# A DiT block on one core: x2 kept in the output tensor, DRAM sums released by weight loads, one more quarter by seven products, ten more constant matmuls

## The chip, the cores and the metric

The kernel runs on one core of a Trainium2 chip. The metric is the device time in microseconds of one execution. A core has a matrix engine (TensorE, PE in the profile), a vector engine (VectorE, DVE), a scalar engine (ScalarE, ACT), a general engine (GpSimd, POOL) and a queue engine (SyncE, SP). SP, ACT and POOL issue transfers. Each engine works through its own list of instructions in order and waits on semaphores that the others raise.

## What is computed

The input x has 2048 rows of 1024 values in bfloat16. One block with conditioned layer norms is applied: linear attention, then a gated feed-forward layer with 3584 hidden columns.

```python
mod = (_silu(c) @ w_mod).reshape(c.shape[0], 6, 1, -1)
sa, ca, ga, sb, cb, gb = (mod[:, 0].copy(), ...)
h = _layernorm(x, axis=-1) * (1 + ca) + sa
x = x + ga * _A_ref(h, A_wqkv, A_wo)          # linear attention, 32 heads
h = _layernorm(x, axis=-1) * (1 + cb) + sb
x = x + gb * _B_ref(h, B_w_gate, B_w_up, B_w_down)
# _B_ref: _gelu(x @ w_gate) * (x @ w_up) @ w_down
```

The x after the attention is called x2 in the kernel; the last line adds the gated feed-forward result to it.

## The kernel before, in words

**Stages.** The rows are taken in four blocks of 512 (TG), and in the feed-forward part in two groups of 1024 (g = 0 and 1). In order of time: the front (`start_phase`, to about 30 us: layer norm of the first block, the modulation columns, the first values of V), K, V and Q with the attention sums (`kvq_phase`, `merge_phase`), the output projection (`wo_phase`), then gate_up(0), down_out(0), gate_up(1), down_out(1). In the profile gate_up(0) lies at about 237 to 407 us, down_out(0) at 403 to 487, gate_up(1) at 482 to 657, down_out(1) from 653 to the end.

**Seven products.** Most products of matrices cut both operands into quarters and form the result from seven quarter products in place of eight, with sums of quarters (s1 to s4 of the activations, t1 to t4 of the weights) prepared beforehand. Some of the seven are cut once more in the same way; they are called nested.

**The down stage.** `down_out(g)` forms seven products with the quarters b11, b21, b22 of w_down and with sums of these quarters, t0 to t3. `nested(name, ...)` does one of them by seven smaller products of 98 matmuls of 256 columns in all (line 2015); `plain(name, ...)` does it directly with 56 matmuls of 512 columns (line 1966) from one load of the whole quarter. In group 0 t1, t2 and t3 are plain, in group 1 only t3 is. `W_AT` (line 1912) names the place in SBUF of each piece, in units of 3.5 KB, and so which earlier piece must be done before a load can be issued. `added` makes the result tile and its `send`, an accumulating store that GpSimd issues (line 1936): it adds to x2. `c22_out`, `c22_quads`, `c21_out`, `c21_last`, `u2_out` are what VectorE does with each finished part in PSUM.

**x2.** `wo_tile` and `wo_stages` write x2 to four DRAM tiles, `x2_scr` (line 766), which `late_norm` reads for group 1's layer norm and `send` adds to. When all eight pieces of a half are sent, line 1942 copies that half, 1 MB, from `x2_scr` to the output; there are three such copies, since the last half is read back (`rest`, line 1950), finished in SBUF and stored by ScalarE's queue (`store`, line 1955).

**Sums in DRAM.** The nested quarters need sums of pieces of w_down. Those of b21, b22 and t0 are made on VectorE (`wd_sums`), that of b11 too (`wd_first`). Those of t2 and t1 (`LATER[1:]`) are made by GpSimd's transfers alone: a plain transfer and then accumulating ones into `v_scr`, eight moves of 448 KB for each (`wd_later`, line 1400). `wd_moves(seen_of, n)` (line 1346) paces them: GpSimd copies one element of `seen_of` into `seen`, which waits until that tile is written and until the last matmul recorded so far is done, and issues the next n moves. Before the change all sixteen are recorded in gate_up(1), two a unit, with `seen_of` in the unit's s1, which VectorE writes.

**Units of gate_up.** A unit is 512 columns of w_gate or w_up, 14 in a group: a load of 1 MB (line 1688), sums on VectorE, matmuls at lines 1729 and 1740. While unit n is multiplied, unit n + 1 (`w_next`) is loaded and summed.

**Order.** Nothing is issued as it is written. `Plan` records all operations, orders them by a planner, and then moves each engine's instructions by the list `SHIFTS` (one number for each instruction: how far it is moved). `Plan.lines` (line 238) tells which bytes an operation touches, which gives the dependences; DRAM scratch is told apart in pieces of 512 elements, inputs and outputs not at all.

**Front.** `keep_warm(n)` (line 900) issues n matmuls of a constant with 512 columns, whose result nobody reads. `scale_cols` (line 930) forms scale columns from w_mod by 32 matmuls of one column, whose weights come in two loads; `scale_wv` multiplies the weights of V by them on VectorE (line 916), and `v_plain` (line 924) multiplies.

Of the kernel before, what the change touches and what calls it, by code (L numbers as in the profile page):

```python
# [11 lines left out]
BF16 = mybir.dt.bfloat16  # L12
F16 = mybir.dt.float16
AF = mybir.ActivationFunctionType
ALU = mybir.AluOpType
# [194 lines left out]

class Op:
    __slots__ = ("extra", "eng", "fn", "args", "kw", "line", "cost", "bytes", "table", "preds", "succs", "early", "late", "due", "ready", "wait", "lat", "needs",
                 "start", "done", "n", "load", "ahead")

class Plan:

# [2032 lines left out]
```

## Time and profile before

| | us |
|---|---|
| median of 3 runs | 738.51 |
| lowest and highest | 737.21, 738.55 |
| the profiled execution's own time | 738.93 |
| its span, first to last instruction | 737.1 |
| granted TensorE clock, mean | 0.996 |

In the lists below a row begins with its start and length in us, or with the stretch and its length; then the engine, the line of the kernel, the operation, what it writes and reads, how many were merged (x), and in brackets the idle time of the engine ahead of it with what ended it. "PEld" is the loading of weights into TensorE, "SPq", "ACTq" and "POOLq" are the sequencers that issue transfers.

### The profile page before, as it was taken

To read this page: it belongs to the slowest core of one execution; us is meant where nothing else is said; L and a number is where in the kernel's file an instruction comes from. 1 tells how busy PE (TensorE), PEld (TensorE's weight loads), DVE (VectorE), ACT (ScalarE), POOL (GpSimd) and SP (SyncE) were. 2 spreads that over 40 slices of the span, in tenths; PEclk is the share of its full clock that TensorE was granted. 3 is DMA by queue.
4 is the path that set the end of the run, shared out by engine and by line. 5 is a ranking of instruction groups with operands and counts; after the bars stand their busy time and mean duration, and the time that the engine had idled before them with its cause. 6 is when DMAs were issued, how large, how long until landed. Compare 5 with 4: busy or idle time off the path is not lost.

```text
span 737.1 us, 12351 instructions
## 1 busy us (share of the span) xinstructions
PE 721.4 (98%) x4463; PEld 413.0 (56%) x4463; DVE 652.3 (88%) x1442; ACT 460.2 (62%) x838; POOL 132.0 (18%) x205
## 2 busy tenths in 40 slices
PE   8999999999999999999999999999989999999996
PEld 4344445444444555555555877455545555568884
DVE  5699998889799999999999994887787999989997
ACT  5486566679687799999877632036757777651220
POOL 2242715011031032222110000131222200000110
PEclk9999999999999999999999999999999999999999
DMA  9877569989999797577968997676869733599987
GB/s 310 298 209 232 139 142 188 325 314 280 314 276 266 264 264 242 188 212 216 235 205 215 265 283 236 196 139 202 190 153 195 144 103 115 159 259 280 284 256 199
DMA packets 177277, 165.70 MB, mean 225 GB/s; under 512 B 34768, under 2 KB 157776, under 8 KB 176656
## 3 DMA queue, kind: packets, MB, share of 16 engines
q1 hardware_dynamic: 150208, 120.08, 55.8%
q0 software_dynamic: 25440, 43.52, 23.7%
q10 hardware_dynamic: 1568, 1.31, 0.6%
q8 instruction: 35, 0.57, 0.3%
q14 instruction: 26, 0.21, 0.1%
HBM read 130.68 MB, written 44.70 MB: 238 GB/s over the span
## 4 chain that ended last, share of the span: by engine, by line
PE 87%; DMA 6%; DVE 4%; issue 1%; POOL 1%; ACT 0%; SPq 0%; DVEq 0%
PE psum L1729 31%; PE psum L2015 13%; PE psum L1740 10%; PE psum L1157 7%; PE psum L1227 6%; PE psum L1966 5%; PE psum L1256 3%; PE psum L1609 3%; PE psum L1543 3%; DVE mem L789 3%; PE psum L924 2%; DMA mem<-in_B_w_up_dram 2%; DMA mem<-ts 1%; DMA mem<-in_B_w_gate_dram 1%; DMA mem<-in_B_w_down_dram 1%; DMA mem<-in_w_mod_dram 1%
## 5 line engine op out<-in xcount | busy, mean ns | idle before, releaser
L789 DVE TENSOR_TENSOR mem<-mem 128x256 f16<-128x256 f16 (+14 forms) x823 | 374.4, 498 | 16.3 <-DMA mem<-in_B_w_up_dram 3.8
L1729 PE MATMUL psum<-mem 128*128 128x512 f16 x1144 | 272.1, 379 | 0.0
L1094 ACT ACTIVATE mem<-psum 128x512 f32<-128x512 f32 (+3 forms) x324 | 170.0, 554 | 116.5 <-PE psum L2015 41.7
L789 DVE TENSOR_TENSOR mem<-psum,mem 128x512 f16<-128x512 f32 (+5 forms) x221 | 164.7, 752 | 31.7 <-ACT mem L1094 11.7
L1729 PEld LDWEIGHTS <-mem 128*128 128x128 f16 (+1 forms) x1144 | 111.8, 98 | 104.2 <-issue 0.6
L2015 PE MATMUL psum<-mem 128*128 128x256 f16 (+1 forms) x980 | 108.6, 273 | 0.0
L1740 PE MATMUL psum<-mem 128*128 128x256 f16 x742 | 105.1, 273 | 3.5 <-DVE psum L789 3.5
L2015 PEld LDWEIGHTS <-mem 128*128 128x128 f16 x980 | 95.9, 98 | 13.0
L1740 PEld LDWEIGHTS <-mem 128*128 128x128 f16 (+1 forms) x742 | 72.5, 98 | 43.5 <-issue 4.4
L1157 PE MATMUL psum<-mem 128*128 128x512 f16 (+1 forms) x280 | 63.3, 379 | 0.7 <-ACT mem L1094 0.7
L1785 ACT ACTIVATE psum<-psum 128x512 f32<-128x512 f32 x56 | 32.8, 586 | 45.8 <-PE psum L1729 33.9
L1936 POOL DMA_DIRECT2D x2s<-mem x12 | 15.6, 1496 | 210.9 <-DVE mem L789 207.2
L789 DVE TENSOR_TENSOR psum<-psum,mem 128x256 f32<-128x256 f32 x106 | 44.9, 429 | 9.4 <-ACT mem L1094 6.9
L1227 PE MATMUL psum<-mem 128*128 128x512 f16 x224 | 51.8, 379 | 0.0
L1966 PE MATMUL psum<-mem 128*128 128x512 f16 (+2 forms) x252 | 49.6, 355 | 1.0 <-DMA mem<-ts 1.0
L1157 PEld LDWEIGHTS <-mem 128*128 128x128 f16 x280 | 26.8, 98 | 32.8 <-DVE mem L1053 1.3
L1804 ACT ACTIVATE mem<-psum 128x512 f16<-128x512 f32 x56 | 33.4, 599 | 8.0 <-PE psum L1729 7.8
L1966 PEld LDWEIGHTS <-mem 128*128 128x128 f16 x252 | 23.5, 98 | 25.1 <-issue 1.2
L1227 PEld LDWEIGHTS <-mem 128*128 128x128 f16 (+1 forms) x224 | 21.5, 98 | 25.6 <-issue 1.0
L1814 ACT ACTIVATE mem<-mem 128x512 f16<-128x512 f16 x56 | 34.8, 630 | 0.0
L1256 PE MATMUL psum<-mem 128*128 128x512 bf16 x128 | 29.5, 379 | 1.0 <-DVE mem L1029 0.8
L1543 PE MATMUL psum<-mem 128*128 128x512 f16 x128 | 28.4, 379 | 0.0
(148 smaller groups left out, 619.4 us busy)
## 6 DMA issues: line engine op xcount, KB each, us to landing
mem<-in_B_w_gate_dram SPq DMA_DIRECT2D x14, 1024.0 KB, 5.4
mem<-in_B_w_up_dram SPq DMA_DIRECT2D x14, 1024.0 KB, 5.1
mem<-in_w_mod_dram SPq DMA_DIRECT2D x24, 512.0 KB, 6.5
mem<-us SPq DMA_DIRECT2D x24, 448.0 KB, 6.8
mem<-in_B_w_down_dram SPq DMA_DIRECT2D x18, 448.0 KB, 6.8
ts<-in_B_w_down_dram POOLq DMA_DIRECT2D x28, 256.0 KB, 5.9
mem<-vs SPq DMA_DIRECT2D x16, 448.0 KB, 6.7
mem<-ts SPq DMA_DIRECT2D x4, 1792.0 KB, 11.7
```

The lines of the kernel that those rows point to most:

```text
L789: ve.tensor_tensor(out=out, in0=a, in1=b, op=op)
L1094: ac.activation(out=t, in_=ps, func=AF.Copy)
L1157: te.matmul(ps, lhsT=A[:, k, i * P:(i + 1) * P], rhs=B[:, k, :], start=(start and k == 0), stop=(k == KH - 1), skip_group_check=True)
L1227: te.matmul(o, lhsT=W[:, k, (j0 + i) * P:(j0 + i + 1) * P], rhs=h_form(a, k), start=(start and k == 0), stop=(k == KH - 1), skip_group_che ...
L1256: te.matmul(ps, lhsT=hr1[b][:, k, tl * P:(tl + 1) * P], rhs=Wk[:, k, n * NW:(n + 1) * NW], start=(k == 0), stop=(k == KD - 1))
L1543: te.matmul(psw[:, half, :], lhsT=pqT[b][:, g, tl * P:(tl + 1) * P], rhs=Wp[:, g, half * NW:(half + 1) * NW], start=(g == 0), stop=(g == K ...
L1729: te.matmul(ps, lhsT=a[:, k, e, :], rhs=b[:, k, :], start=(start and k == 0), stop=(k == KH - 1), skip_group_check=True)
L1740: te.matmul(ps, lhsT=self.x[a][:, k, :], rhs=self.y[y][:, k, :], start=(start and k == 0), stop=(k == KH // 2 - 1), skip_group_check=True)
L1804: ac.activation(out=o, in_=ps, func=AF.Gelu_apprx_tanh)
L1814: ac.activation(out=o, in_=o, func=AF.Gelu_apprx_tanh)
L1966: te.matmul(psm[:, b, c], lhsT=A[:, i, q * P:(q + 1) * P], rhs=wt[:, i, c], start=(start and i == 0), stop=(i == NPR - 1), skip_group_chec ...
L2015: te.matmul(ps[:, q, :], lhsT=a[:, k, q * P:(q + 1) * P], rhs=y[:, k, :], start=(start and q == 0 and k == 0), stop=(k == NPR // 2 - 1), s ...
```

## The change

x2 is kept in the output: the four views that `wo_tile`, `wo_stages`, `late_norm`, `send` and `rest` use are rows of the output tensor, and the copies go. The planner now tells the output apart in pieces of 128 elements. In group 0 t2 is nested, as it is in group 1 already: the sums of A21 go to three places at 144 KB (`sub_d`), `c22_quads` gets a `send`, and t3 adds the part that `c22_quads` leaves in `p5v`. A plain quarter is loaded in two halves. The eight moves for t2 are recorded in gate_up(0) and the eight for t1 in gate_up(1), one a unit at the units in `MOVE_AT`, with `seen_of` in the raw weights of the next unit, which SP's load writes. `keep_warm(2)` becomes `keep_warm(8)`, and a `keep_warm(4)` is added behind the scale columns. `SHIFTS` is another list for every engine, so that all engines have another order in most stages.

```diff
-        if name.startswith("in_") or name.startswith("out_"):
+        if name.startswith("in_"):
             got = ()
         else:
-            unit = 512 * isz
+            unit = (P_OUT if name.startswith("out_") else 512) * isz
...
+    sub_d = [at(144 + 3.5 * j, [NPR // 2, HB], F16) for j in range(3)]
...
-    x2_scr = [scr_pool.tile([TG, D], BF16, name=f"x2s{b}", tag=f"x2s{b}") for b in range(NG)]
+    x2_scr = [o_dram[b * TG:(b + 1) * TG, :] for b in range(NG)]
...
-        keep_warm(2)
+        keep_warm(8)
         scale_cols(0, 0, KH, psc[0])
         scale_cols(0, KH, KD, psc[0])
+        keep_warm(4)
         start_tile(1, xh[1])
...
+    MOVE_AT = ((0, 1, 2, 3, 4, 5, 6, 11), (1, 2, 3, 4, 5, 6, 7, 8))
...
-            if g and n == 0:
-                wd_todo.extend(wd_later())
-            if g and n:
-                wd_moves(w["s1"][:, 0, 0, 0:1], 2)
-            if g == 0 and n % 2 == 0:
-                if n and n // 2 + EARLY - 1 < NPR // 2:
-                    fill += wd_sums(n // 2 + EARLY - 1)
-                wd_moves(w["s1"][:, 0, 0, 0:1], 2)
+            if n == 0:
+                wd_todo.extend(wd_later(LATER[g + 1]))
+            if n in MOVE_AT[g]:
+                wd_moves(w_next["a11"][:, 0, 0, 0:1], 1)
+            if g == 0 and n % 2 == 0 and n and n // 2 + EARLY - 1 < NPR // 2:
+                fill += wd_sums(n // 2 + EARLY - 1)
...
-             "b22": (7, 8, 9, 10, 4, 5, 6), "t2": 0, "t3": 11},
+             "b22": (10, 1, 2, 7, 8, 9, 6), "t2": (3, 4, 0, 5, 10, 1, 2), "t3": 11},
...
-                sent[half] += hi - lo
-                if sent[half] == 2 * TT:
-                    r = (2 * g + half) * TG
-                    gp.dma_start(out=o_dram[r:r + TG, :], in_=x2_scr[2 * g + half])
...
-            sy.dma_start(out=wt, in_=wd_full[name])
+            for c in (slice(0, NPR // 2), slice(NPR // 2, NPR)):
+                sy.dma_start(out=wt[:, c], in_=wd_full[name][:, c])
...
         def u2_out(q, ps, c):
-            t = w12[:, q, :]
-            tt_op(t, p5v[:, q, :], ps, ALU.subtract)
-            tt_op(t, t, gbrow[:, NW:D], ALU.mult)
+            tt_op(p5v[:, q, :], p5v[:, q, :], ps, ALU.subtract)
+            tt_op(w12[:, q, :], p5v[:, q, :], gbrow[:, NW:D], ALU.mult)
...
-        def c22_quads(x2, x1):
+        def c22_quads(x2, x1, send=None):
...
+                if send is not None:
+                    tt_op(quad(x2, r, c), t, gate2(1, c), ALU.mult)
+                    if (r, c) in ((1, 0), (0, 1)):
+                        send(2 * r, 2 * r + 2)
+                    return
...
         def c21_out(xt, send):
             def out(q, ps, c):
-                finish(xt, 0, q, ps, None)
+                t = c0_ring()
+                tt_op(t, ps, gbrow[:, 0:NW], ALU.mult)
+                tt_op(xt[:, q], t, p5v[:, q, :], ALU.add)
...
-            m7 = plain("t2", A21, c22_out(*added(1, 1)), False)
-            run(*m7[:2], n3[5], *m7[2:4], n3[6], *m7[4:])
-            run(*plain("t3", A22, c21_out(*added(1, 0)), False))
+            sub_sums(A21, sub_d, None, [slice(0, NPR // 2)])
+            x2, send = added(1, 1)
+            n7 = nested("t2", A21, sub_d, None, c22_quads(x2, None, send))
+            run(n7[0], n3[5], n7[1], n3[6], *n7[2:5])
+            m8 = plain("t3", A22, c21_out(*added(1, 0)), False)
+            run(m8[0], n7[5], m8[2], n7[6], m8[1], *m8[3:])
```

`wd_later(name)` is now given one name and returns its eight moves, in the order o0, o0 +=, o2, o1, o2 +=, o1 +=, o3, o3 +=.

More of the change, by code (lines that the diff above doesn't have):

```diff
@@ L213 @@
                  "start", "done", "n", "load", "ahead")
+P_OUT = 128
 class Plan:
@@ L1398, in wd_first, with wd_later @@
         gp.dma_start(out=v_scr[:, c, 0], in_=v)
-    def wd_later():
-        todo = []
-        for name in LATER[1:]:
-            v = v_scr[:, :, LATER.index(name)]
-            w = wd_full[name].rearrange("p (i e) (h n) -> p e h i n", e=2, h=2)
-            o0, o1, o2, o3 = (v[:, :, f] for f in range(4))
-            todo.append([(o0, w[:, 0, 0], 0), (o2, w[:, 0, 1], 0), (o0, w[:, 0, 1], 1), (o2, w[:, 1, 1], 1),
-                         (o1, o0, 0), (o1, w[:, 1, 1], 1), (o3, o1, 0), (o3, w[:, 1, 0], 1)])
-        a, b = todo
-        return [*a[:2], *b[:2], *a[2:4], *b[2:4], *(m for pair in zip(a[4:], b[4:]) for m in pair)]
+    def wd_later(name):
+        v = v_scr[:, :, LATER.index(name)]
+        w = wd_full[name].rearrange("p (i e) (h n) -> p e h i n", e=2, h=2)
+        o0, o1, o2, o3 = (v[:, :, f] for f in range(4))
+        return [(o0, w[:, 0, 0], 0), (o0, w[:, 0, 1], 1), (o2, w[:, 0, 1], 0), (o1, o0, 0), (o2, w[:, 1, 1], 1),
+                (o1, w[:, 1, 1], 1), (o3, o1, 0), (o3, w[:, 1, 0], 1)]
     def kvq_phase():
@@ L1938, in send @@
                     in_=xt[:, lo:hi], accum_op=ALU.add)
-                sent[half] += hi - lo
-                if sent[half] == 2 * TT:
-                    r = (2 * g + half) * TG
-                    gp.dma_start(out=o_dram[r:r + TG, :], in_=x2_scr[2 * g + half])
             return xt, send
-        sent = [0, 0]
         def rest(half, nh, xt=None):
@@ L2047, in nested @@
             return [g1, g2, g3, g4, g5, g6, g7]
-        def finish(xt, nh, q, ps, sb, op=ALU.add):
-            gb = gbrow[:, nh * NW:(nh + 1) * NW]
-            if sb is not None:
-                t = c0_ring()
-                tt_op(t, sb, ps, op)
-                ps = t
-            tt_op(xt[:, q], ps, gb, ALU.mult)
         def quad(v, r, c):
@@ L2126, in c12_out @@
             return out
-        def c22_out(xt, send):
-            def out(q, ps, c):
-                finish(xt, 1, q, ps, p5v[:, q, :], ALU.subtract)
-                if q % 2:
-                    send(q - 1, q + 1)
-            return out
-        def c22_quads(x2, x1):
+        def c22_quads(x2, x1, send=None):
             def out(r, c, ps, sb, op):
```

355 rows, old and new, of the table SHIFTS are left out of this document.

## The prediction

> **What bounds the kernel now.** I read first the page's busy shares and the chain of waits, then busy time by stretch, then the few rows in which TensorE stands still.
>
> ```profile
> span 737.1 us, 12351 instructions
> PE 721.4 (98%) x4463; PEld 413.0 (56%) x4463; DVE 652.3 (88%) x1442; ACT 460.2 (62%) x838; POOL 132.0 (18%) x205
> PE 87%; DMA 6%; DVE 4%; issue 1%; POOL 1%; ACT 0%; SPq 0%; DVEq 0%
> ```
>
> ```profile
> 20.00:40.00 20.00, 18.98 (x111) 7.72 (x110) 13.81 (x36) 11.08 (x17) 6.74 (x14) 1.00 0.76 262
> 40.00:90.00 50.00, 49.34 (x274) 23.53 (x273) 47.88 (x118) 32.93 (x47) 22.42 (x41) 1.00 0.71 195
> 165.00:230.00 65.00, 64.72 (x340) 28.91 (x339) 57.85 (x102) 52.21 (x84) 11.92 (x20) 1.00 1.00 283
> 230.00:405.00 175.00, 174.51 (x994) 96.90 (x993) 169.89 (x428) 150.25 (x300) 29.90 (x45) 1.00 0.78 229
> 405.00:457.00 52.00, 51.02 (x425) 41.37 (x424) 44.52 (x76) 23.38 (x38) 0.00 (x0) 1.00 0.94 266
> 457.00:510.00 53.00, 53.00 (x275) 26.69 (x273) 39.59 (x87) 14.22 (x31) 10.61 (x11) 1.00 0.68 178
> 510.00:585.00 75.00, 72.02 (x419) 40.74 (x418) 61.62 (x153) 52.50 (x113) 21.46 (x22) 1.00 0.77 174
> 655.00:714.00 59.00, 59.00 (x536) 52.29 (x535) 58.26 (x90) 13.73 (x25) 2.47 (x2) 1.00 1.05 289
> ```
>
> Each row gives a stretch and its length, then busy time of PE, PEld, DVE, ACT and POOL, the granted clock, the share of the DMA engines and GB/s. From 20 us on TensorE lacks 1.02 + 0.66 + 0.28 + 0.49 + 0.98 + 2.98 = 6.41 us in the rows shown that have a gap. The program is bound by its matmuls; a gain is either a matmul less, one of these gaps, or the two ends. VectorE is the second limit: 97% in gate_up(0) (169.89 of 175) and 99% in the last down stage (58.26 of 59).
>
> **The change part by part.** The sum is made against the profiled execution's 738.93 us, that is its span and 1.8 us around it; it lies 0.42 us above the median, 738.51, and that is taken off at the end.
>
> *(a) t2 of group 0 by seven products.* The plain quarter is 4 x 14 = 56 matmuls of 512 columns; nested it is 7 x 14 = 98 of 256.
>
> ```profile
> 457.26 24.17 PE psum L1966 x112
> 656.48 56.56 PE psum L2015 x518
> ```
>
> One takes 24.17/112 = 0.216 us, the other 56.56/518 = 0.109 us. 98 x 0.1092 = 10.70 replaces 56 x 0.2158 = 12.08: **-1.38 us**, nearly certain, since TensorE has no gap in 457 to 510.
>
> VectorE pays for it. The instructions by shape rise by three 128x1792 and one 128x7x256 sum, ten half-precision or gate operations of 512 elements and one that reads PSUM.
>
> ```profile
> L789 DVE TENSOR_TENSOR mem<-mem 128x512 f16<-128x512 f16 x18 | 8.2, 481 | 0.4
> L789 DVE TENSOR_TENSOR mem<-mem 128x1792 f16<-128x1792 f16 x7 | 7.4, 1087 | 0.1
> L789 DVE TENSOR_TENSOR mem<-psum,mem 128x512 f16<-128x512 f32 x6 | 4.1, 685 | 6.9 <-ACT mem L1094 6.9
> ```
>
> 4 x 1.09 + 10 x 0.48 to 0.69 + 0.69 = 9.8 to 11.9 us. The cover is VectorE's idle time in 457 to 510, 53.00 - 39.59 = 13.4 us, and 7.5 us in the stretch before. It fits with little over, and gate_up(1) begins behind it; without the cover it would be 11.9 us late. I take **+0.3**, bounds 0 and +3 (a quarter of it falling in the wrong place).
>
> *(b) x2 in the output.* Three copies from x2s to the output go (line 1942, 1 MB each); nothing computes less. One copy leaves mid-kernel. The other two stand at the end:
>
> ```profile
> 724.07 0.53 POOL L1942 DMA_DIRECT2D out_dram<-x2s  x1 [4.59 <-DMA x2s<-mem]
> 728.73 3.52 ACTq L1955 DMA_DIRECT2D out_dram<-mem  x1
> 728.73 5.99 ACTq L1955 DMA_DIRECT2D out_dram<-mem  x6
> 731.75 0.29 DVE L789 TENSOR_TENSOR mem<-mem 128x128 bf16<-128x128 f16 x1
> L1955 ACTq DMA_DIRECT2D out_dram<-mem x8: 388/416/3521, 723.6 to 734.3; - x8
> out_dram<-x2s POOLq DMA_DIRECT2D x3, 8.1
> ```
>
> A store is normally issued in 0.42 us. One takes 3.52, from 728.73 to 732.25, and 724.07 + 8.1 = 732.2 is where the copy lands. The four stores behind it wait on ScalarE's queue: VectorE's last result is there at 732.04, the last issue ends at 734.72. Without the long issue the last could end at 732.04 + 0.39 = 732.43, 2.29 us sooner. The changed order makes a 512-wide piece the last but one, whose two VectorE operations (2 x 0.69, the 128x512 row under (a)) outlast the 14 matmuls of a quarter of the width behind it (14 x 0.216 / 4 = 0.76) by 0.62 us; 2.29 - 0.62 = 1.67, and that piece's own store may hold up the last issue. I take **-1.4**, bounds 0 (the issue is long for another reason) and -2.3.
>
> *(c) The DRAM sums.* Before, all 16 moves for t2 and t1 run in gate_up(1), two a unit, released by VectorE's s1. After, 8 run in gate_up(0), 8 in gate_up(1), one a unit, released by the landing of the next weights.
>
> ```profile
> L1335 POOL DMA_DIRECT2D vs<-ts x12: 934/1482/1780, 497.5 to 583.4; - x12
> L1335 POOL DMA_DIRECT2D vs<-vs x4: 752/756/1507, 546.8 to 573.7; - x4
> vs<-ts POOLq DMA_DIRECT2D x12, 448.0 KB, 7.0
> 510.67 0.37 SPq L1688 DMA_DIRECT2D mem<-in_B_w_gate_dram  x1
> mem<-in_B_w_up_dram SPq DMA_DIRECT2D x14, 1024.0 KB, 5.1
> 523.24 11.93 DMA mem<-in_B_w_up_dram
> 535.19 0.29 DVE L789 TENSOR_TENSOR mem<-mem 128x256 f16<-128x256 bf16 x1 [2.66 <-DMA mem<-in_B_w_up_dram]
> 537.15 0.38 PE L1740 MATMUL psum<-mem 128*128 128x256 f16 x2 [2.24 <-DVE psum L789]
> 557.41 2.48 DVE L789 TENSOR_TENSOR mem<-mem 128x1024 f16<-128x1024 bf16 x6 [1.16 <-DMA mem<-in_B_w_up_dram]
> 560.29 0.60 PE L1740 MATMUL psum<-mem 128*128 128x256 f16 x4 [0.75 <-DVE psum L789]
> q0 software_dynamic: 8608, 7.60, 43.0%
> ```
>
> A weight load that lands in 5.1 us took 11.93 with the moves in flight; VectorE waited 2.66 and TensorE 2.24 behind it, then 0.75 at 560. A load that starts after a single move should not meet three. I take 2.4 of these 2.99 us: **-2.4**, bounds 0 and -3.
>
> gate_up(0) gets the load instead. The last row is POOL's queue over 500 to 600 us: 43 us of 16 engines for 7.60 MB, the size of 17 moves of 448 KB, 2.5 us each. Eight more are 20 us on 175, the DMA share goes from 0.78 to 0.89. VectorE has 5.1 us of idle time there, so a load that comes late is not caught up. Behind the new waits on POOL stand the stores of xhs, us and ts, whose buffers VectorE needs a unit later. I take **+0.5**, bounds 0 and +9 (seven waits such as the 1.16).
>
> *(d) t1 of group 0 loaded in two halves.*
>
> ```profile
> 437.30 3.18 PE L1966 MATMUL psum<-mem 128*128 128x512 f16 x14 [0.98 <-DMA mem<-ts]
> ```
>
> Every matmul group starts with the first half, which can start and land sooner; **-0.9** of 0.98, bounds 0 and -1.
>
> *(e) Ten more constant matmuls in front.* Three now lie before tile 0's transposes, three before scale_cols, four between its halves (its order on TensorE: 16 products, 4 constants, 16 products).
>
> ```profile
> 30.70 1.50 PE L1256 MATMUL psum<-mem 128*128 128x512 bf16 x5 [0.77 <-DVE mem L1029]
> 9.71 0.95 PE L933 MATMUL psum<-mem 128*128 128x1 bf16 x32 [1.90 <-DMA mem<-in_w_mod_dram]
> 11.27 1.14 DVE L916 TENSOR_SCALAR mem<-mem 128x512 f16<-128x512 bf16 x4 [0.41 <-DMA mem<-in_A_wqkv_dram]
> 7.33:10.75 3.42, 1.52 (x45) 1.35 (x43) 1.65 (x7) 1.92 (x7) 0.00 (x0) 1.00 1.08 370
> 10.75:14.16 3.41, 3.41 (x15) 1.46 (x13) 2.78 (x10) 1.88 (x4) 0.00 (x0) 0.50 1.10 348
> ```
>
> A stretch in which TensorE was busy for 1.52 of 3.42 us is followed by one at half clock. With the gap filled that stretch runs at full speed: at most 3.41/2 = 1.7 us. Against that stand the four constants that hold up the second half, 4 x 0.216 = 0.86 us, of which 0.41 is covered by VectorE's wait for the weights: best -1.25. If the clock still halves, the four cost 4 x 0.43 = 1.7 less 0.41: +1.3. And 40 to 90, where VectorE is 96% busy, may swallow a gain. I take **-0.6**, nearer the filled gap because some 2.7 of 3.42 us would be busy.
>
> The Trainium skill (TensorE: Matmul & The Clock Gate, "What's actually happening") says that the clock halves after an idle window of about 3.4 us, full clock needs a busy one, and the window runs freely from the kernel's start. The trace agrees on the length (3.41 us) but not on idle: a window busy for 44% was enough. By that rule the place of the window can differ between executions, and the term could be 0 in some of them.
>
> *(f) The rest* is a new order on all engines with the same durations: 0, bounds -1.9 (the gaps in 20 to 230, 1.02 + 0.66 + 0.28) and +2.
>
> Sum: -1.38 + 0.3 - 1.4 - 2.4 + 0.5 - 0.9 - 0.6 = -5.88; 738.93 - 5.88 - 0.42 = **732.6 us**.
>
> **The rivals.**
>
> *Only half arrives.* VectorE, with 10 us more in down_out(0) and fully busy at the end, gives back what TensorE gains: (a), (d) and (e) show up again as waits at gate_up(1)'s start. Left are (b) and (c): 738.51 - 3.8 + 0.8 = 735.5. For: the 96 to 99% above. Against: 13.4 us of idle time where the work is added.
>
> *Slower: gate_up(0) becomes bound by late weights.* The eight moves make loads late where VectorE has 3% to spare. At 1.16 us for each of seven units, 732.6 - 0.5 + 8.1 = 740.2; with the price of 2.24 seen at 537, up to 748. It decides from 6.4/7 = 0.9 us a unit on. For: 11.93 us in 510 to 585 at a DMA share of only 0.77. Against: the moves there were in flight when the load began; now a load's landing releases the move, and the next load starts some 12 us later (510.67, then 523.24), while a move lands in 7.0.
>
> *The change does not do what it says.* The long issue has another cause, and one move a unit still meets the loads: left is (a) and (d), taken back in part by VectorE: 738.51 - 1.4 = 737.1, or no change.
>
> **How the numbers follow.** Forecast 0.61 (its own range 730 to 735), half 0.17, slower 0.13, nothing 0.09. All terms at their best are 738.51 - 1.38 - 2.3 - 3 - 1 - 1.25 - 1.9 = 727.7, which will not all come; the low end is 728.5. The high end, 740, takes in the half and the nothing and the foot of the slower case. About 0.2% (1.5 us) is what a measurement of this kernel tells from no change. Faster 0.78, same 0.09, slower 0.13.
>
> **What would show it.** (a) 98 more L2015-type matmuls and no new gap in 457 to 510. (b) no issue of a store above 1 us, the last ending within 2 us of VectorE's last result. (c) weight loads of group 1 near 5 us and no idle time of TensorE above 0.5 us in 510 to 585; in 230 to 405 not over 1.5 us idle. (d) no wait for ts at t1. (e) granted clock 1.00 in the window after 10.75. It is wrong if TensorE's idle time in gate_up(0) exceeds 6 us, or if the front is later than before by the first matmul of line 1256, now at 30.7 us.

## The result, and the profile after

The changed kernel takes 729.23 us (median of four, 728.97 to 730.43) against 738.53 us (median of four, 737.21 to 738.97): a ratio of 0.988, interval 0.9863 to 0.9897. The forecast was 732.6 us with a range of 728.5 to 740; the gain is 9.3 us where 5.9 were forecast. The time lies inside the range, 0.8 us below the 730 to 735 that the forecast named as its own. The execution profiled took 729.17 us. Over the 58 executions of before and 16 of after that were measured in the end, the medians differ by 7.8 us (737.38 and 729.59): the sum started from a profile of 738.93 us, 1.55 us above the median of those 58, and part of the surplus belongs to that.

The page of the profile after: its head, the busy shares, the chain of waits, and from its costliest groups the two kinds of matmuls of the down stage.

```profile
span 727.4 us, 12503 instructions
PE 717.1 (99%) x4504; PEld 417.8 (57%) x4515; DVE 662.3 (91%) x1457; ACT 461.5 (63%) x841; POOL 133.3 (18%) x210
...
PE 94%; DVE 2%; POOL 2%; ACT 1%; issue 1%; DMA 0%; DVEq 0%; ACTq 0%
...
L2008 PE MATMUL psum<-mem 128*128 128x256 f16 (+1 forms) x1078 | 119.6, 273 | 0.0
...
L1959 PE MATMUL psum<-mem 128*128 128x512 f16 (+2 forms) x196 | 38.0, 349 | 0.0
```

TensorE's share of the chain rises from 87 to 94%, the share of transfers falls from 6% to nothing. The nested product is there: 1078 matmuls of 256 columns, 98 more than before. VectorE has 10 us more to do (662.3 for 652.3), as forecast. Of 4515 weight loads 4504 have a matmul in the trace: 11 records are missing, all of lines 1160 and 1259, ahead of 165 us.

Busy time by stretch after, with the columns of the rows before (length, PE, PEld, DVE, ACT, POOL, clock, DMA share, GB/s):

```profile
230.00:405.00 175.00, 175.00 (x1005) 97.98 (x1003) 170.35 (x431) 151.76 (x303) 45.25 (x61) 1.00 0.92 245
405.00:457.00 52.00, 52.00 (x416) 40.50 (x414) 49.95 (x81) 21.46 (x35) 1.28 (x1) 1.00 1.02 271
457.00:510.00 53.00, 53.00 (x333) 32.31 (x331) 48.56 (x103) 18.97 (x39) 8.88 (x9) 1.00 0.78 193
510.00:585.00 75.00, 75.00 (x437) 42.63 (x436) 64.07 (x158) 55.04 (x118) 11.23 (x14) 1.00 0.54 135
655.00:714.00 59.00, 59.00 (x523) 50.86 (x521) 57.75 (x87) 11.86 (x21) 4.89 (x4) 1.00 0.97 259
```

In these rows TensorE has no gap left. The moves have gone from one stage to the other: the DMA share falls from 0.77 to 0.54 in 510 to 585 and rises from 0.78 to 0.92 in 230 to 405, and in neither does TensorE wait. In 457 to 510 VectorE's idle time shrinks from 13.4 to 4.4 us, and TensorE stays full.

The end of the program after: VectorE's last two pieces, and then all eight stores of ScalarE (shortest, median and longest issue in ns).

```profile
722.53 0.69 DVE L791 TENSOR_TENSOR mem<-psum,mem 128x512 f16<-128x512 f32 x1 [0.23 <-PE psum L1959]
...
724.38 0.29 DVE L791 TENSOR_TENSOR mem<-mem 128x128 bf16<-128x128 f16 x1
```

```profile
L1947 ACTq DMA_DIRECT2D out_dram<-mem x8: 338/382/460, 717.9 to 724.7; - x8
```

No issue takes longer than 0.46 us, where one took 3.52. VectorE ends at 724.67, the last issue starts at 724.7 and the span ends at 727.4. Before, 2.7 us lay between VectorE's last result and the end of the last issue; now it is 0.4.

The front of both kernels, by the stretches of 3.41 us in which the granted clock is kept (those of after start at 4.13 us), and the first K matmul:

```profile
4.13:7.54 3.41, 2.26 (x11) 0.73 (x9) 2.83 (x8) 2.31 (x6) 0.64 (x3) 1.00 0.93 314
7.54:10.96 3.42, 3.35 (x56) 2.49 (x57) 2.77 (x11) 2.09 (x8) 0.00 (x0) 1.00 1.07 369
10.96:14.37 3.41, 3.35 (x22) 1.59 (x20) 2.72 (x10) 3.15 (x7) 0.00 (x0) 1.00 1.11 350
```

```profile
29.50 3.83 PE L1259 MATMUL psum<-mem 128*128 128x512 bf16 x16 [0.95 <-DMA mem<-in_A_wqkv_dram]
```

No stretch is at half clock. The first K matmul starts 1.20 us sooner than at 30.70, and now waits for the weights.

Where the 9.7 us of span went, by these rows and those of before:

| place | before | after | difference | forecast |
|---|---|---|---|---|
| start to first K matmul | 30.70 | 29.50 | -1.20 | -0.6 (e) |
| PE missing in 230 to 405 (gate_up(0)) | 0.49 | 0.00 | -0.49 | +0.5 (c) |
| PE missing in 405 to 457 (t1) | 0.98 | 0.00 | -0.98 | -0.9 (d) |
| t2's matmuls, 98 x 0.109 for 56 x 0.216 | 12.08 | 10.70 | -1.38 | -1.38 (a) |
| waits for VectorE's extra work | 0 | 0 | 0 | +0.3 (a) |
| PE missing in 510 to 585 (gate_up(1)) | 2.98 | 0.00 | -2.98 | -2.4 (c) |
| end of the last matmul to end of span | 5.79 | 4.12 | -1.67 | -1.4 (b) |

Together -8.70. Most of the other 1.0 us lies in the same places. The profile shows a wait as the idle time behind the end of the matmul before it, and these ends are modelled: a matmul of 512 columns is listed with 0.379 us in the traces, while the next one starts 0.216 us after it, so that each wait is shown some 0.16 us too short. Counted from start to start, less the 0.216 or 0.109 us that a matmul takes, TensorE in the two traces loses 0.67 us less in 243 to 400, 1.12 less in 400 to 480 and 3.43 less in 480 to 585. With -1.20, -1.38 and -1.67 that is -9.47, and some -0.2 us is left for (f), for which 0 was forecast within -1.9 to +2.

### The profile page after: what moved, and what is told of

The parts are those of the page before. It is cut to its first block, busy times and chain, and to the rows that moved or that the text cites. A ratio compares the mean times of both kernels' runs of the same rounds, so it can differ in the third digit from the quotient of the medians.

```text
span 727.4 us, 12503 instructions
## 1 busy us (share of the span) xinstructions
PE 717.1 (99%) x4504; PEld 417.8 (57%) x4515; DVE 662.3 (91%) x1457; ACT 461.5 (63%) x841; POOL 133.3 (18%) x210
## 4 chain that ended last, share of the span: by engine, by line
PE 94%; DVE 2%; POOL 2%; ACT 1%; issue 1%; DMA 0%; DVEq 0%; ACTq 0%
PE psum L1728 34%; PE psum L2008 16%; PE psum L1739 11%; PE psum L1160 7%; PE psum L1230 7%; PE psum L1959 5%; PE psum L1542 4%; PE psum L1608 3%; PE psum L1259 2%; PE psum L926 2%; PE psum L1274 1%; POOL mem L877 1%; PE psum L808 1%; DVE mem L791 1%; DMA mem<-in_A_x_dram 0%
## 5 line engine op out<-in xcount | busy, mean ns | idle before, releaser
L791 DVE TENSOR_TENSOR mem<-mem 128x512 f16<-128x512 f16 (+11 forms) x837 | 383.4, 501 | 11.4 <-ACT mem L1097 2.3
L791 DVE TENSOR_TENSOR mem<-psum,mem 128x512 f16<-128x512 f32 (+5 forms) x225 | 167.2, 750 | 24.4 <-PE psum L1160 4.8
L2008 PE MATMUL psum<-mem 128*128 128x256 f16 (+1 forms) x1078 | 119.6, 273 | 0.0
L2008 PEld LDWEIGHTS <-mem 128*128 128x128 f16 x1078 | 105.5, 98 | 14.3
L1934 POOL DMA_DIRECT2D out_dram<-mem x12 | 14.6, 1414 | 218.3 <-DVE mem L791 218.3
L1160 PEld LDWEIGHTS <-mem 128*128 128x128 f16 x280 | 27.2, 98 | 33.0 <-issue 1.6
L1959 PE MATMUL psum<-mem 128*128 128x512 f16 (+2 forms) x196 | 38.0, 349 | 0.0
L1338 POOL DMA_DIRECT2D ts<-in_B_w_down_dram x28 | 27.6, 1165 | 11.1 <-DMA ts<-in_B_w_down_dram 11.0
```

The costliest lines, as they stand in the source:

```text
L791: ve.tensor_tensor(out=out, in0=a, in1=b, op=op)
L1160: te.matmul(ps, lhsT=A[:, k, i * P:(i + 1) * P], rhs=B[:, k, :], start=(start and k == 0), stop=(k == KH - 1), skip_group_check=True)
L1959: te.matmul(psm[:, b, c], lhsT=A[:, i, q * P:(q + 1) * P], rhs=wt[:, i, c], start=(start and i == 0), stop=(i == NPR - 1), skip_group_chec ...
L2008: te.matmul(ps[:, q, :], lhsT=a[:, k, q * P:(q + 1) * P], rhs=y[:, k, :], start=(start and q == 0 and k == 0), stop=(k == NPR // 2 - 1), s ...
```

## The experiments

In all kernels made from before or after every instruction not named keeps the place that it has on its engine there. Three chips were used; each run is set beside executions of before on its own chip. Those 58 executions of before spread from 733.37 to 740.34 us, median 737.38, and 16 of after from 728.95 to 733.59, median 729.59, so that differences under 1 us between kernels are read from their traces.

**The copies at the end.**

```diff
 # before, down_out
-                if sent[half] == 2 * TT:
-                    r = (2 * g + half) * TG
-                    gp.dma_start(out=o_dram[r:r + TG, :], in_=x2_scr[2 * g + half])
```

> The kernel before without its three copies of 1 MB from x2s to the output; those three halves of the output are left out. Theory (a store's issue on ScalarE's queue is long because a copy is in flight): no store issue above 0.5 us, the last one ends about 0.4 us after VectorE's last result instead of 2.7 us, and the time is 738.5 - 2.3 = 736.2 us. Rival (the issue is long for a reason of its own): one issue of some 3.5 us stays, and the time is 738.2 to 738.5 us.

Measured: 736.24 us against 737.67, ratio 0.9982 (0.9966 to 0.9999). ScalarE's stores by the trace of this kernel:

```profile
L1955 ACTq DMA_DIRECT2D out_dram<-mem x8: 351/412/479, 723.6 to 732.1; - x8
```

The long issue is gone with the copies alone. VectorE's last result is there at 731.97, the last issue ends at 732.48, and from the end of the last matmul to the end of the span 3.59 us pass for 5.79 before: the 2.2 us of the theory, in the trace. Two kernels described next, b_landing and b_halves, have the copies; in their traces the longest issue is 2.4 and 2.7 us:

```profile
L1955 ACTq DMA_DIRECT2D out_dram<-mem x8: 388/432/2362, 720.6 to 730.3; - x8
```

```profile
L1955 ACTq DMA_DIRECT2D out_dram<-mem x8: 389/417/2661, 720.1 to 729.9; - x8
```

With before's own trace that makes three, and in each the long issue ends 0.2 us before the copy has landed by the semaphore events (at 732.25 and 732.44, 728.08 and 728.25, 727.84 and 728.01). So its length is no property of the store: it is what the copy still has to go.

**t1 in halves.**

```diff
 # b_halves: before with this; a_onepiece: after with t1 undone
-            sy.dma_start(out=wt, in_=wd_full[name])
+            for c in (slice(0, NPR // 2), slice(NPR // 2, NPR)):    # t1 alone
+                sy.dma_start(out=wt[:, c], in_=wd_full[name][:, c])
```

> The kernel before with the plain load of t1 of group 0 in two halves, nothing else changed. Theory (each matmul group starts with the first half, which lands sooner): the wait for ts of 0.98 us before the first t1 matmul shrinks to 0.2 us or less, and the time is 738.5 - 0.8 to 1.0 = 737.6 us. Rival (VectorE has the next turn: it is busy for 44.5 of the stage's 52 us): the wait returns behind t1 or at gate_up(1)'s start, and the time is 738.3 to 738.7 us.

> The changed kernel with the plain load of t1 of group 0 in one piece again. Theory: the wait for ts at the first t1 matmul returns, 0.8 to 1.1 us, and nothing catches it up: 730.2 us. Rival (in the new order the buffer is free sooner, or VectorE sets the pace of the stage): 729.0 to 729.5 us.

Measured: b_halves 737.40 us against 737.67, ratio 0.9995 (0.9976 to 1.0015), which decides nothing; a_onepiece 730.46 us (730.08 to 736.62), against 729.26 and 730.33 for after itself on two chips. The traces decide. The first t1 matmul in b_halves, and then in a_onepiece:

```profile
434.21 3.19 PE L1967 MATMUL psum<-mem 128*128 128x512 f16 x14
```

```profile
435.24 3.18 PE L1959 MATMUL psum<-mem 128*128 128x512 f16 x14 [1.17 <-DMA mem<-ts]
```

With halves there is no wait for ts, in one piece it is back with 1.17 us. Nothing shows in its place: in b_halves PE has no gap from 405 to 510, and a_onepiece loses nothing more behind it.

**The DRAM sums.** Two things change at once in (c): the number of moves in a unit of gate_up(1), two or one, and what releases them. The four combinations are before, after, and these two:

```diff
 # b_landing: before (two a unit)
-                wd_moves(w["s1"][:, 0, 0, 0:1], 2)
+                wd_moves(w_next["a11"][:, 0, 0, 0:1], 2)
 # a_s1: after (one a unit)
-                wd_moves(w_next["a11"][:, 0, 0, 0:1], 1)
+                wd_moves(w["s1"][:, 0, 0, 0:1], 1)
```

> The kernel before with one thing changed: the 16 moves for t2 and t1 still run in gate_up(1), two a unit, but each pair is released by the landing of the next unit's weights in place of VectorE's s1. Theory (what counts is whether moves are in flight when a weight load starts): the waits of TensorE at 537 and 560 us go, and the time is 738.5 - 2.4 to 3.0, some 735.8 us. Rival (what counts is how many moves there are: a pair needs up to 14 us, a new load starts every 12): loads stay late, TensorE still loses 2 to 3 us in 510 to 585, and the time is 738.0 to 739.5 us.

> The changed kernel with its moves, one a unit in both groups, released by VectorE's s1 as before in place of the landing of the next weights. Theory (the release counts): moves are in flight when weight loads start, gate_up(1) loses 1 to 3 us again and gate_up(0), where VectorE has 3% to spare, more: 731 to 738 us. Rival (their number counts, one a unit leaves room): 729.0 to 729.7 us and no gap above 0.3 us in 510 to 585.

> The changed kernel with its moves released by VectorE's s1, a second time: six times of the first run lay between 728.95 and 732.54 us, and the execution profiled was the fastest of them. Theory (the release counts, though not in every execution): the times spread again over 3 us above 728.9, and an execution above 730.5 us shows a weight load above 8 us and a wait of TensorE of 0.5 us or more behind it in gate_up(0) or gate_up(1). Rival (the spread came from the front): a profile above 730.5 us has its loss ahead of 40 us and no gap in the two stages.

Measured: b_landing 735.21 us against 737.67, ratio 0.9969 (0.9953 to 0.9986); a_s1 731.16 us (728.95 to 732.54) and, on another chip, 729.65 us (728.93 to 731.79) beside 730.33 (729.57 to 733.59) for after on that chip. The stretch of gate_up(1) where before lost 2.98 us, in b_landing and in a_s1_again:

```profile
510.00:585.00 75.00, 74.61 (x435) 42.33 (x433) 64.38 (x158) 53.84 (x116) 19.77 (x21) 1.00 0.76 172
```

```profile
510.00:585.00 75.00, 75.00 (x438) 42.65 (x436) 64.15 (x158) 55.06 (x118) 11.68 (x13) 1.00 0.56 135
```

Pairs released by a landing lose 0.39 us; single moves released by s1 lose nothing. In these executions each remedy does nearly all of it by itself. By these traces the rival "their number counts" is wrong for pairs and right for single moves, and the theory "the release counts" the other way about. The events of the trace show how. In before two moves are issued at 520.49 and 521.23 and a store of x2 at 521.96; the load at 523.24 begins with all three in flight, a further move follows at 526.95, and the load lands at 535.17. In b_landing the pair is issued at 516.37 and 517.13 and lands by 523.85, as the load at 523.10 has just begun; the next pair and a store follow at 524.33 to 525.80, while the load is under way, and it lands at 528.17 all the same, after 5.1 us. In a_s1_again a load of 541.88 meets one move issued at 540.82 and lands after 8.1 us, which is soon enough.

For single moves released by s1 the times do not settle it. The median of the first run, 731.16 us, lies in the range of the theory (731 to 738), and four of its six executions took over 730.5; that of the second, 729.65, lies in the rival's. Neither trace of a_s1 was of an execution above 730.5 us (728.95 and 728.97, the fastest of its run and the second), so where the later executions lose, in these two stages or elsewhere, stays open.

Then the other side: how much room gate_up(0) has for moves.

```diff
 # a_double: after; idle_scr is 448 KB of DRAM that nobody reads
-                wd_todo.extend(wd_later(LATER[g + 1]))
+                wd_todo.extend(m for mv in wd_later(LATER[g + 1]) for m in (mv, (idle_scr, t2_part, 0))[:2 - g])
-                wd_moves(w_next["a11"][:, 0, 0, 0:1], 1)
+                wd_moves(w_next["a11"][:, 0, 0, 0:1], 2 - g)
```

> The changed kernel with one more DRAM copy of 448 KB, from ts to a place that nobody reads, behind each of the eight moves in gate_up(0). Theory (moves that a landing releases are hidden there, with room for as many again): 729.2 to 730.2 us, PE's busy time in 230 to 405 stays above 174.5. Rival (the eight moves fill the room that there was: the DMA share there is 0.92, and 20 us more on 175 would make it 1.03): weight loads late, VectorE cannot catch up with 4.65 us to spare, eight waits of 1.16 us: 738 us.

Measured: 737.29 us (733.93 to 742.77), 7.7 us over after's median. The rival holds, to within 1 us. Busy time in the stage, the waits of PE and DVE in it (what waited, for what, us in total, times, longest), and two stretches of the clock that lie in it:

```profile
230.00:405.00 175.00, 169.65 (x955) 93.74 (x953) 163.50 (x415) 146.52 (x293) 52.10 (x69) 0.99 0.95 257
```

```profile
PE psum L1739 <- DVE psum L791: 5.3, 4, 2.9
...
DVE mem L791 <- DMA mem<-in_B_w_up_dram: 3.5, 2, 3.1
```

```profile
384.06:387.47 3.41, 0.77 (x5) 0.34 (x4) 1.46 (x3) 1.87 (x5) 0.39 (x1) 1.00 1.47 310
387.47:390.88 3.41, 3.18 (x11) 1.58 (x11) 2.80 (x7) 0.43 (x2) 1.65 (x3) 0.50 1.00 194
```

TensorE waits 5.3 us for VectorE, which waits for weights: the chain of the prediction's slower rival, load, then VectorE, then TensorE. It is not eight equal waits of 1.16 but four with one of 2.9, and the stall is followed by a stretch at half clock, which adds up to 1.7 (half of 3.41). So eight moves are free there, and eight copies of the same size behind them cost 7.7 us.

**The constant matmuls in front.**

```diff
 # a_noconst: after without all ten; a_no4: without the four between the halves
-        keep_warm(8)
+        keep_warm(2)
...
-        keep_warm(4)
```

> The changed kernel without the ten added constant matmuls in front (three ahead of tile 0's transposes, three ahead of scale_cols, four between its halves); all else in its order. Theory (they keep the clock up): a stretch of 3.4 us at half clock between 7 and 17 us, the first K matmul 1 us later than 29.5 us, time 729.2 + 1.0 to 1.7 = 730.5 us. Rival (the first K matmul waits for the wqkv weights, 0.95 us of it in the changed kernel, so that the front is bound by the load whatever the clock does): first K matmul at 29.5 us or sooner, time 729.0 to 729.5 us.

> The changed kernel without the four constant matmuls between the halves of the first scale_cols; the other six that were added stay. Theory (the four fill a stretch that is otherwise too empty): the mean clock falls below 0.999 in most executions as it did without all ten (0.994 to 0.998), and the time is 730 to 731 us. Rival (the six are enough, and the four, 0.86 us of work, only hold up the second half): clock 0.999 to 1.000 and 728.4 to 728.9 us.

Measured: a_noconst 731.04 us (729.98 to 732.32), 1.5 us over after's median, with a mean clock of 0.994 to 0.998 in each of its four executions. Its ratio to before, 0.9907 to 0.9941, overlaps those of after on the other two chips (0.9866 to 0.9912 and 0.9893 to 0.9933), so the clock and the trace have to tell. The first K matmul is a poor mark here: in a_noconst a single one starts at 29.12 us, sooner than after's 29.50 as the rival has it, and the next ones only at 30.32. The last eight products of V are a better one, in after and then in a_noconst:

```profile
26.66 1.89 PE L926 MATMUL psum<-mem 128*128 128x512 f16 x8
```

```profile
27.39 1.89 PE L926 MATMUL psum<-mem 128*128 128x512 f16 x8
```

Without the ten they come 0.73 us later (the other two traces of after have 26.48 and 26.64), and the end of the last matmul is 0.80 us later too (724.08 for 723.28). a_no4 took 729.63 us (728.84 to 730.59) beside 730.33 for after on that chip, clock 0.999 to 1.000 in all five. The ten keep the clock up, and six of them are enough. Without the four the same products of V start at 26.10 us, 0.4 to 0.6 sooner than in the three traces of after, but the first K matmul only at 29.16, behind a wait of 1.17 us for its weights, so that most of it is lost again.

The execution of a_no4 that was profiled, its slowest, loses time elsewhere: a weight load issued at 478.45 us, as the stores of down_out(0) run, takes 8.1 us (5.1 in after), and TensorE waits 1.0 us at 488, at the start of gate_up(1).

The clock's stretches start at another time in each execution: the first one recorded starts at 7.33 us in before and at 4.13 us in after, and in the other twelve traces in between, all within one length of 3.41 us. One pair has the same phase: before (7.33, shown with the prediction) and a_s1 (7.32), which has all ten constants. Then a_noconst, and then b_halves, which has before's front:

```profile
7.32:10.73 3.41, 3.40 (x52) 2.08 (x51) 2.88 (x8) 2.42 (x7) 0.00 (x0) 1.00 1.08 372
10.73:14.15 3.42, 3.39 (x31) 1.93 (x28) 3.13 (x12) 3.02 (x6) 0.00 (x0) 1.00 1.10 348
```

```profile
6.50:9.91 3.41, 1.87 (x43) 1.40 (x42) 3.26 (x10) 3.17 (x11) 0.00 (x0) 1.00 1.05 365
9.91:13.33 3.42, 3.42 (x19) 2.02 (x18) 2.50 (x10) 2.45 (x4) 0.00 (x0) 0.50 1.10 358
```

```profile
4.26:7.67 3.41, 2.17 (x15) 0.85 (x13) 3.38 (x9) 2.87 (x7) 0.53 (x3) 1.00 1.07 365
7.67:11.09 3.42, 2.64 (x45) 1.83 (x46) 2.81 (x12) 2.50 (x9) 0.00 (x0) 1.00 1.09 358
```

At equal phase 1.52 us of matmuls in the stretch were followed by half clock, 3.40 were not; the first K matmul came at 30.70 and 29.45, though these two kernels also differ in their order. In b_halves the gap falls across two stretches, with 2.17 and 2.64 us, and neither is followed by half clock; its first K matmul starts at 28.79 us, sooner than the 29.50 of after at nearly the same phase (4.13), so in an execution of that phase the constants have nothing to gain.

Over many executions: of the 58 of before 56 had a mean clock of 0.991 to 0.998, of 16 of after 15 had 0.999 or 1.000. Over the 58 the time falls by 0.46 us for 0.001 of clock (correlation -0.52), and the means are 0.9964 and 0.9994: 3.0 x 0.46 = 1.4 us, an estimate for (e), and rather too high, since a stall costs both time and clock, as the next part shows.

**The changed kernel again.**

> The changed kernel once more, as the mark for the runs that take parts of it away: 729.2 us, and a granted clock of 1.00 in front if the clock's window lies in every execution as in the one profiled; if the window's place differs between executions, a half clock somewhere before 15 us and up to 1 us more in some of the times.

> The changed kernel as the mark for the runs beside it: 729.2 us, clock 0.999 to 1.000 in every execution.

Measured: 729.26 us (728.95 to 729.96), and on another chip 730.33 us (729.57 to 733.59), where the profile shows the execution of 733.59, with clock 0.997. In it TensorE lost 2 us at 414 us, in the first matmuls of down_out(0). Its row, the last accumulating move of gate_up(0), and the clock's stretches there:

```profile
416.40 4.79 PE L2008 MATMUL psum<-mem 128*128 128x256 f16 x27 [2.01 <-DMA mem<-vs]
```

```profile
394.55 1.54 POOL L1338 DMA_DIRECT2D vs<-ts  x1 [7.37 <-DMA vs<-vs]
```

```profile
413.85:417.26 3.41, 1.40 (x13) 1.02 (x12) 2.52 (x5) 1.78 (x3) 0.00 (x0) 1.00 1.16 308
417.26:420.67 3.41, 3.41 (x18) 2.45 (x17) 1.89 (x3) 1.81 (x4) 0.00 (x0) 0.50 1.12 295
```

The same move in the execution of after profiled first:

```profile
391.27 1.54 POOL L1338 DMA_DIRECT2D vs<-ts  x1 [4.08 <-DMA vs<-vs]
```

The last of the eight moves is released late (MOVE_AT has 11 as its last unit), waits on GpSimd for the move ahead of it, and runs while the down stage's first loads do. The move ahead is issued 1.26 us later, takes 12.74 us for 10.72, and lands at 394.02 instead of 390.74 us. The last one, issued 3.28 us later, lands at 407.40 instead of 400.82, the fourth load of vs behind it at 416.36 instead of 413.46, and the stall of 2.01 us brings a stretch at half clock. 2.0 + 1.7 = 3.7 us, and 733.59 less 3.7 is 729.9. Why the move ahead is later and slower in this execution stays open, and so does whether the other execution above 733 us, not profiled, had the same cause.

**A better order.** Traces of after show three places where something ready stands behind something that waits.

```diff
 # a_order: after, the order on TensorE (VectorE and the stores follow in the third)
-    ... 8 of L1274 (wait 0.7), 4 of L1160, ...
+    ... 4 of L1160, 8 of L1274, ...
-    ... 4 of L1160 (wait 0.5), 20 of L1274, ...
+    ... 20 of L1274, 4 of L1160, ...
-    last quarter: 128, 256, 512, 128 columns
+    last quarter: 512, 256, 128, 128 columns
```

> The changed kernel in another order at three places, with the same instructions: four matmuls of line 1160 ahead of the eight of line 1274 that wait at 60 us, twenty of line 1274 ahead of the four of line 1160 that wait at 82 us, and the 512-wide piece of the last quarter ahead of its three narrow ones, as before. Theory (each of the three is a wait that other work can fill): less 0.7, 0.4 and 0.3 us, 727.8 us. Rival (VectorE is busy for 47 of the 50 us from 40 to 90 and for the last 10 us, so that the waits come back a little later): 729.0 to 729.5 us.

Measured: 728.47 us (728.15 to 730.54), beside 730.33 for after on the same chip. Four of its five times lie below the lowest of the 16 of after, 728.95; the intervals of the two ratios, 0.9871 to 0.9906 and 0.9893 to 0.9933, just overlap. The place at 60 us in after_3, then in a_order, and then the stretch of both:

```profile
60.63 0.62 PE L1274 MATMUL psum<-mem 128*128 128x129 f16 x8 [0.71 <-DVE mem L791]
61.09 1.02 PE L1160 MATMUL psum<-mem 128*128 128x512 f16 x4
```

```profile
59.79 1.03 PE L1160 MATMUL psum<-mem 128*128 128x512 f16 x4
60.67 0.62 PE L1274 MATMUL psum<-mem 128*128 128x129 f16 x8
```

```profile
40.00:90.00 50.00, 47.94 (x268) 23.39 (x267) 46.67 (x118) 32.60 (x48) 23.97 (x42) 1.00 0.67 196
```

```profile
40.00:90.00 50.00, 49.06 (x273) 23.90 (x272) 48.25 (x120) 32.93 (x49) 24.05 (x42) 1.00 0.68 196
```

The first two swaps give 1.12 us, as expected, and VectorE, at 97% of the stretch, does not take it back there. The third gives 0.13 us where 0.3 was expected: from the end of the last matmul to the end of the span 3.99 us for 4.12. In the execution traced some 0.8 us, counted from start to start, is lost again at 486 to 492 us, at the start of gate_up(1), where a weight load takes 7.3 us for 5.1 in after; whether the new order brings that load on was not tried, and a_no4 has the same wait without it. By its times the kernel beats both, before by 9 us and after by 1 to 2, with intervals that overlap.

## Why the prediction was right, point by point

- **(a) t2 nested.** Right, as far as the trace of after shows; no run takes it away alone. The work falls by what the two durations give, and the starts of the narrow matmuls in after are 0.109 us apart too. The cover held with 4.4 us to spare, so the 0.3 us put on VectorE's work did not arise.
- **(b) The copies.** Right in mechanism: the issue is long because the copy is in flight, and it is gone with it (b_nocopy). Five stores stood behind it, not the four that were counted. -1.67 in the trace for -1.4. Of the 0.62 us deducted for the order of the last pieces, a_order shows 0.13 to be due to it; b_nocopy's end is shorter than after's by 0.53 us (3.59 for 4.12), and the rest of that was not tried.
- **(c) The DRAM sums.** Right in place and direction, mis-sized in both stages, and the largest part of the miss. "I take 2.4 of these 2.99": all of it went. The reason was given as one, a single move and its release; the traces show two, each of which does it nearly alone, so the sum had a reserve that the prediction did not count (single moves released by s1 were traced only near 729 us). Its sign, weight loads near 5 us, did not hold throughout: of the seven issued in 500 to 585 in after three take 9.3, 7.3 and 7.1 us, and no wait of TensorE follows. "I take +0.5, bounds 0 and +9" for gate_up(0): it was -0.49, outside the bounds. Eight moves at a DMA share of 0.92 cost nothing there, and the gaps of before, 0.65 us between two matmuls at 369 us the largest, are gone; which part of the change removed them was not tried. The slower rival was sound in its mechanism and its price, though not in its number: with eight copies more it comes, at 737.3 us for the 740 that it named.
- **(d) t1 in halves.** Right: -0.98 for -0.9, and it comes and goes with the halves alone.
- **(e) The constants.** Right in mechanism; the size stays open. Before and after, which differ in their order too, give -1.20 in the first profile, -1.25 at equal phase and some -1.4 over many executions; the ten alone, by a_noconst, are worth 0.7 to 0.9 us in the traces and 1.5 in the medians, against -0.6 with a bound of -1.25. The prediction halved the gain for the four constants that hold up the second half. They do, by 0.4 to 0.6 us in the trace of a_no4 for its 0.86 less 0.41, but the wait for the weights of K hides most of it, and no gain in time can be told from nothing. That the place of the stretch differs between executions was stated with the Trainium skill (TensorE: Matmul & The Clock Gate, "What's actually happening"), and the traces agree: 14 starts, spread over 3.20 us. The consequence drawn from it, that the term could be 0 in some executions, holds in b_halves.
- **(f) The new order.** Right as far as it goes: 0 was forecast, some -0.2 is left over for it. TensorE misses 2.16 us of 40 to 90 in after and 0.66 in before, and makes that up elsewhere ahead of 243 us. The trace of after has new waits at 60 to 82 us, which a_order takes away, so the order is better in some places and worse in these.
- **"Only half arrives"** fell: no wait appears at gate_up(1)'s start in the traces of after. The 1.0 us in a_no4 and less in a_order show that there is little to spare at this place: a weight load is late ahead of both. **"The change does not do what it says"** fell with b_nocopy and b_landing.

The sum took something off nearly every term, and nearly every term came whole: 729.23 us stands 1.5 us above the 727.7 of all terms at their best. No errors cancelled here; nearly all went one way, and what was taken off, in (c) above all, was too much.

Not foreseen was the changed kernel's own weak place, the late last move into down_out(0), which costs 3.7 us in one of three profiles of it.

## What to carry to other kernels

When two remedies for one collision go in together, price the loss as gone, and test each alone, with traces of its longer times too. In this kernel a transfer had a price only where it met another: eight moves were free at a DMA share of 0.92 and eight copies more cost 7.7 us, and one that came 3.3 us late at the seam of two stages cost 3.7. One profile is one execution: where a stall depends on a phase or on transfers that meet, compare many times and several traces before a term of 1 us is sized.

## What the runs showed of the hardware

- The issue of a store on ScalarE's queue took 2.4 to 3.5 us while a DRAM copy of 1 MB issued by GpSimd was in flight, ended within 0.2 us of its landing in three traces, and took at most 0.51 us in the eleven traces without the copy.
- The granted clock was halved for one stretch of 3.41 us after stretches in which matmuls filled 0.77 (a_double), 1.40 (after_3), 1.43 (b_landing), 1.52 (before), 1.87 (a_noconst) and 2.08 us (b_nocopy) of it, and was kept after stretches with 1.67 (a_onepiece, at 722.75 us), 1.92 (b_halves, at 529.91), 1.98 (before, at 532.93), 2.17 (b_halves) and 2.26 us (after). By this measure the border lies somewhere between 1.5 and 2.1 us and is not sharp; an idle stretch is not needed. It happens in the middle of the program too, at 387 us in a_double and at 417 in after_3.
